# V of the memory rows turned by transposing DMA, attention's last blocks emptied in one step, and two zero loads on SyncE's queue

## The chip, the cores and the metric

The kernel runs on one NeuronCore of a Trainium2 chip; the other cores are idle. The metric is the device time of that core in microseconds, as the median of several executions. Five engines work side by side, each through its own list of instructions, in order: TensorE (PE, matrix products, with the weight loads shown apart as PEld), VectorE (DVE), ScalarE (ACT), GpSimd (POOL) and SyncE (SP, which here only issues DMA transfers). DMA transfers can also be issued from ACT and from POOL; all of them are carried by the same 16 DMA engines.

## The reference, cut to what matters

Two independent parts are computed and their outputs laid side by side. Part A is a state-space layer: a complex linear recurrence over 2048 steps between two matrix products. Part B is attention with a recurrent memory: the 2048 rows of x are cut into 64 segments of 32, and each segment attends to its own rows and to 8 memory rows, which are the first 8 output rows of the segment before.

```python
mem = mem0
for s in range(n_seg):                                   # 64 segments
    xs = x[:, s*32:(s+1)*32, :]
    h = concatenate([mem, xs], axis=1)                   # 8 + 32 rows
    q, k, v = (einsum('btd,dhe->bhte', h, W) for W in (Wq, Wk, Wv))   # 32 heads of 128
    p = softmax(where(mask, q @ k.T * scale, -1e9))
    o = einsum('bhte,hed->btd', p @ v, Wo)
    mem = o[:, :8, :]
    outs.append(o[:, 8:, :])
```

The kernel does not run the segments one after another. It guesses the memory rows from means of x, computes all segments at once with them, and tests at the end whether the guess was within a tolerance; a branch with a plain loop stands ready for inputs where it was not, and is not taken here. "Memory rows" below are the 73 guessed rows (66 of them one to three for each group of three segments, and 7 for the first).

## The kernel before: the parts that the change touches

V of all rows is kept in DRAM, in `vx` for the rows of x and in `vt` for the memory rows, one pair of tensors for each group `hb` of four heads, with ones in 8 columns behind each head's 128 (`EW` is 136, `E` is 128). For the memory rows V comes out of the projection with the head's 128 columns on the partitions (`vm`), so it has to be turned before it is stored. TensorE does that, VectorE copies the result out of PSUM into a staging tile, and two transfers store it:

```python
def v_mem(self, hb, w=None):
    w = w or self.load_wv(hb)
    p = k.ps("P")
    for h in range(4):
        for c in range(KC):                               # 8
            k.PE.matmul(p[:, h*NM:(h+1)*NM], w[:, c, h*128:(h+1)*128], self.memT[:, c, :], ...)
    vm = self.vmp.tile([128, 4, NM], BF16, name="b_vm", bufs=1)         # NM is 73
    k.copy("v", vm[:], p[:, 0:4*NM]...)
    yield
    pt = k.ps("P", (128, 1024), BF16)
    for h in range(4):
        k.PE.transpose(pt[0:NM, h*128:(h+1)*128], vm[:, h, :], k.ident[:])
    st = self.next_st()                                   # one of two staging tiles b_vst
    k.copy("v", st[0:NM, 0, :, 0:E], pt[0:NM, 0:512]...)
    sv = st[:, 0, :, :].rearrange("p h e -> p (h e)")
    k.SP.dma_start(self.vx[hb][64:64+NMX, :], sv[0:NMX, :])             # 7 rows
    k.SP.dma_start(self.vt[hb][:], sv[NMX:NM, :])                       # 66 rows
    yield
```

`v_mem` is called for the eight groups in turn: for 0 and 1 during the last output blocks of part A (`stage2`, a loop over 32 half blocks of 16 matmuls), for 2 to 7 during attention, at steps 4 and 6 of every second head pair.

Attention walks over 16 head pairs `hp`. For each of 11 steps `u` it makes scores, exponentials and masked weights (`att_front`), and multiplies older weights with V (`att_back`, three blocks at a time), keeping up to 8 blocks behind. V of a head pair is loaded from DRAM into one of two tiles of 128 partitions, of which 99 hold V; the 29 others are filled with zeros once per tile, from a stretch of zeros in DRAM:

```python
def load_v(self, hp):
    vt = self.vts[hp % 2]
    if hp < 2:
        z = self.vx[0][T+32:T+32+128-GW, 0:2*EW].unsqueeze(1).to_broadcast([128-GW, NG, 2*EW])   # 29 x 22 x 272
        k.tc.keep_in_program_order(k.G.dma_start(vt[GW:128, :, :], z))
    ...
    k.tc.keep_in_program_order(k.SP.dma_start(vt[0:GX, :, :], self.vx[hb]...))   # 96 x 22 x 272
    k.SP.dma_start(vt[GX:GW, :, :], self.vt[hb]...)                              # 3 x 22 x 272
    ...

def attention(self):
    ...
    for hp in range(HP):                                  # 16
        for u in range(NU):                               # 11
            if u == 2:
                self.load_v(hp + 1)
            pend += self.att_front(hp, u)
            back(8)
            yield hp, u
    for keep in (6, 3, 0):
        back(keep)
        yield HP, 0
```

Every `yield` of attention is filled with matmuls of other work: with the projections of q and k for the next head pair (`proj`), and at the end with the first output product (`outproj_first`, four matmuls at a time). `V` of head pair 0 is loaded at the end of part A, in `att_init`; the projections of q and k for pair 0 run in between.

Of the kernel before, what the change touches and what calls it, by code (L numbers as in the profile page):

```python
# [9 lines left out]
BF16 = mybir.dt.bfloat16  # L10
# [16 lines left out]
HB = 8; HP = 16  # L27
# [7 lines left out]
NMX = 7  # L35
NM = NTL + NMX
# [3 lines left out]
EW = E + 8  # L40
# [13 lines left out]
class Pinned:  # L54


    def __init__(self, k, name, eng):
        self.k, self.name, self.eng = k, name, eng
# [278 lines left out]
class PartB:  # L337
    def __init__(self, k, x, mem0, Wq, Wk, Wv, Wo, out):
        self.k = k
        self.x, self.mem0, self.out = x, mem0, out  # L340
        self.Wf = [w.rearrange("(c p) h e -> p c (h e)", p=128) for w in (Wq, Wk, Wv)]
        self.Wo = Wo.rearrange("h e d -> e h d")
        self.vx = [k.drp.tile([NSLOT, 4 * EW], BF16, name=f"b_vx{i}") for i in range(HB)]
        self.vt = [k.drp.tile([NTL, 4 * EW], BF16, name=f"b_vt{i}") for i in range(HB)]
        self.on = [k.drp.tile([T, 1024], BF16, name=f"b_on{i}") for i in range(4)]
        self.tn = [k.drp.tile([NR, 1024], BF16, name=f"b_tn{i}") for i in range(4)]
        c = k.cst
        self.m0T = c.tile([128, KC, M], BF16, name="b_m0T")
        self.gx = c.tile([128, KC, NM], BF16, name="b_gx")
        self.vmp = c  # L350
        self.xbar = c.tile([128, KC, NSEG], BF16, name="b_xbar")
        self.ogT = c.tile([128, H, NSEG], BF16, name="b_ogT")
        self.accE = c.tile([128, HP * NU], FP32, name="b_accE")
        self.accR = c.tile([128, HP * 2 * NG], FP32, name="b_accR")
        self.flag = c.tile([1, 1], I32, name="b_flag")
# [184 lines left out]
    def v_mem(self, hb, w=None):  # L540
        k = self.k
        w = w or self.load_wv(hb)
        p = k.ps("P")
        for h in range(4):
            for c in range(KC):
                k.PE.matmul(p[:, h * NM:(h + 1) * NM], w[:, c, h * 128:(h + 1) * 128], self.memT[:, c, :], start=(c == 0), stop=(c == KC - 1))
        vm = self.vmp.tile([128, 4, NM], BF16, name="b_vm", bufs=1)
        k.copy("v", vm[:], p[:, 0:4 * NM].rearrange("p (h n) -> p h n", h=4))
        yield
        pt = k.ps("P", (128, 1024), BF16)  # L550
        for h in range(4):
            k.PE.transpose(pt[0:NM, h * 128:(h + 1) * 128], vm[:, h, :], k.ident[:])
        st = self.next_st()
        k.copy("v", st[0:NM, 0, :, 0:E], pt[0:NM, 0:512].rearrange("p (h e) -> p h e", h=4))
        sv = st[:, 0, :, :].rearrange("p h e -> p (h e)")
        k.SP.dma_start(self.vx[hb][64:64 + NMX, :], sv[0:NMX, :])
        k.SP.dma_start(self.vt[hb][:], sv[NMX:NM, :])
        yield


# [57 lines left out]
    def load_v(self, hp):  # L618
        if hp < HP:
            k = self.k  # L620
            vt = self.vts[hp % 2]
            if hp < 2:
                z = self.vx[0][T + 32:T + 32 + 128 - GW, 0:2 * EW].unsqueeze(1).to_broadcast([128 - GW, NG, 2 * EW])
                k.tc.keep_in_program_order(k.G.dma_start(vt[GW:128, :, :], z))  # L624
            hb, cs = hp // 2, slice((hp % 2) * 2 * EW, (hp % 2) * 2 * EW + 2 * EW)
            k.tc.keep_in_program_order(k.SP.dma_start(vt[0:GX, :, :], self.vx[hb].rearrange("(g p) n -> p g n", p=GX)[:, :, cs]))
            k.SP.dma_start(vt[GX:GW, :, :], self.vt[hb].rearrange("(g j) n -> j g n", j=3)[:, :, cs])
            self.vtile[hp] = vt
# [62 lines left out]
    def attention(self):  # L691
        pend = []

        def back(keep):
            while len(pend) > keep:
                n = min(3, 2 * NG - pend[0][1])
                self.att_back([pend.pop(0) for _ in range(n)])
        for hp in range(HP):
            for u in range(NU):
                if u == 2:  # L700
                    self.load_v(hp + 1)
                pend += self.att_front(hp, u)
                back(8)
                yield hp, u
        for keep in (6, 3, 0):
            back(keep)
            yield HP, 0


    def load_o(self, tb, q, t):  # L710
# [265 lines left out]
def kernel_main(tc, A_x, A_Lre, A_Lim, A_Bre, A_Bim, A_Cre, A_Cim, A_logdt, A_Dskip, B_x, B_mem0, B_Wq, B_Wk, B_Wv, B_Wo, out,  # L976
                force=False, dbg=None):
    with ExitStack() as ctx:
        k = K(tc, ctx)
# [3 lines left out]
        b = PartB(k, B_x, B_mem0, B_Wq, B_Wk, B_Wv, B_Wo, out)  # L983

        def pool(name, side, bufs=2):
            return tc.tile_pool(name=name, bufs=bufs, side=side, reuse_waits="tile")
# [8 lines left out]
        with pool("p1x", "right") as p1x, pool("p1", "right", 1) as p1:  # L995
# [10 lines left out]
            wv = {0: w0, 1: b.load_wv(1)}  # L1006
# [17 lines left out]
            for kind, pc, q in order[1:]:  # L1024
# [3 lines left out]
                if kind == "v":  # L1028
                    b.v_x(pc, q, wv[pc])
                    if q == 3:  # L1030
                        if pc >= 3:
                            b.og(pc, wv[pc])
                        n = (pc + 2) if pc + 2 < PC else (2, 0)[pc + 2 - PC]
# [3 lines left out]
                n = 4 * pc + q  # L1037
# [27 lines left out]
        with pool("p2h", "right") as p2h, pool("p2", "right") as p2:  # L1065
            a.s2_tiles(p2h, p2)
            g = b.guess(p2)
            s2 = a.stage2()
            b.wog = []
            a.load_h(1, nc.scalar)  # L1070
            for i, _ in enumerate(s2):
                if i in (1, 4, 7):
                    n = (2, 0, 1)[(i - 1) // 3]
                    b.og(n, wv[n], "O")
                    if n == 2:
                        wv[1] = b.load_wv(1)
                if i in (3, 7, 11, 15):
                    b.load_wog((3, 7, 11, 15).index(i), p2)
                if i in (9, 11, 13, 15, 17, 19, 21, 22):
                    next(g)  # L1080
                if i == 20:
                    b.load_wqk(0)
                if i == 23:
                    for _ in g:
                        pass
                if i in (26, 28):
                    vm = b.v_mem((i - 26) // 2, wv[(i - 26) // 2])
                if 26 <= i < 30:
                    next(vm)


# [15 lines left out]
        for n, (hp, u) in enumerate(at):  # L1107
            if n == 12:
                k.SP.dma_start(wo0[:], b.Wo[:, :, 0:512])
            if hp % 2 == 0 and 2 < hp + 2 < HP:  # L1110
                if u == 4:
                    vm = b.v_mem(hp // 2 + 1)
                if u in (4, 6):
                    next(vm)
            if hp == 13 and u in (3, 6, 9):
                b.load_o_early(u // 3 - 1)
            want = min(18 * HP, LEAD + (n + 1) * 18 // 11)
            while done < want:
                next(pr)
                done += 1  # L1120
            if done == 18 * HP:
                if first is None:
                    xs.close()
                    b.p4a = ctx.enter_context(pool("p4a", "left", 1))
                    wo1 = b.p4a.tile([128, H, 512], BF16, name="wo1")
                    b.wo = (wo0, wo1)
                    b.load_o_early(3)
                    for h in range(0, H, 16):
                        k.SP.dma_start(wo1[:, h:h + 16, :], b.Wo[:, h:h + 16, 512:D])
                    first = b.outproj_first()  # L1130
                next(first)
# [30 lines left out]
@with_exitstack  # L1162
def kernel(
    ctx: ExitStack,
    tc: tile.TileContext,
    A_x: bass.AP,
    A_Lambda_re: bass.AP,
    A_Lambda_im: bass.AP,
    A_B_re: bass.AP,
    A_B_im: bass.AP,  # L1170
    A_C_re: bass.AP,
    A_C_im: bass.AP,
    A_log_dt: bass.AP,
    A_Dskip: bass.AP,
    B_x: bass.AP,
    B_mem0: bass.AP,
    B_Wq: bass.AP,
    B_Wk: bass.AP,
    B_Wv: bass.AP,
    B_Wo: bass.AP,  # L1180
    B_seg_len: bass.AP,
    out: bass.AP,
):
    assert int(B_seg_len) == SEG
    kernel_main(tc, A_x, A_Lambda_re, A_Lambda_im, A_B_re, A_B_im, A_C_re, A_C_im, A_log_dt, A_Dskip,
                B_x, B_mem0, B_Wq, B_Wk, B_Wv, B_Wo, out)
# [35 lines left out]
```

## Time and profile before

| | |
|---|---|
| median of 3 executions | 1248.88 us (1248.05 to 1248.9) |
| span of the profiled execution | 1246.3 us |
| granted TensorE clock, mean | 0.999 |
| PE busy | 1234.5 us in 8270 matmuls |
| DVE, POOL, ACT busy | 668.1, 283.0, 263.6 us |
| DMA traffic | 176.91 MB, mean 142 GB/s |
| transposes of `b_vm` on PE | 32 |
| zero loads, issued from POOL | 2, of 338.9 KB each |

How it is read: the profile is one execution, seen by a hardware profiler. Matrix products overlap one another, so the busy time of one (its line gives, for instance, 219 ns) is longer than the distance from one start to the next; what a matmul costs is read from the starts in the timeline. A transfer's own line gives the time in which the issuing engine was held by the issue, not the time until the data was there. The DMA column of the window view is the mean busy share of 16 engines.

### The profile page before, as it was taken

Reading aid. Unit: us, or ns where it says so; the run is one execution under the profiler, and the core shown is the slowest. Engines: PE = TensorE matmul, PEld = TensorE weight load, DVE = VectorE, ACT = ScalarE, POOL = GpSimd, SP = SyncE. Lnnn points to the kernel's source line nnn. Section 1 sums busy time; section 2 is a strip of 40 time slices with the busy share of each in tenths; the row PEclk is TensorE's granted clock in tenths of the full one; section 3 lists DMA queues with packets and bytes.
Section 4 is the critical chain, followed back from the end, with each engine's and each line's share of the span. In section 5 each row is a group of like instructions: output and inputs, shape, how many; then the busy total and the mean of one; then the engine's idle time right before and its main releaser. Section 6 shows DMA issues by size and latency. Waiting matters only on the chain.

```text
span 1246.3 us, 20124 instructions
## 1 busy us (share of the span) xinstructions
PE 1234.5 (99%) x8270; PEld 662.3 (53%) x8342; DVE 668.1 (54%) x1250; ACT 263.6 (21%) x631; POOL 283.0 (23%) x409
## 2 busy tenths in 40 slices
PE   9999999999999999999999999999999999999998
PEld 5444444444455555656565656555665554446444
DVE  4688899998711124666666666666666641001000
ACT  5344444443310000211111111111111110000000
POOL 4111331212332332222222222323222320000000
PEclk9999999999999999999999999999999999999999
DMA  9965444553898737764454544545474279407000
GB/s 251 267 194 146 130 139 125 146 153 110 243 319 249 246 105 158 150 155 119 102 144 108 144 108 110 142 89 130 96 153 99 58 223 229 107 18 153 17 17 27
DMA packets 317336, 176.91 MB, mean 142 GB/s; under 512 B 141080, under 2 KB 302480, under 8 KB 317240
## 3 DMA queue, kind: packets, MB, share of 16 engines
q1 hardware_dynamic: 292552, 147.26, 48.4%
q10 hardware_dynamic: 21072, 24.38, 5.9%
q0 software_dynamic: 3616, 3.94, 1.3%
q8 instruction: 66, 1.08, 0.4%
q14 instruction: 30, 0.25, 0.1%
HBM read 89.14 MB, written 53.17 MB: 114 GB/s over the span
## 4 chain that ended last, share of the span: by engine, by line
PE 97%; issue 1%; DMA 1%; POOL 0%; DVE 0%; another core or an unknown queue 0%; ACT 0%; POOLq 0%; DVEq 0%; ACTq 0%
PE psP L64 81%; PE psU L64 9%; PE psS L64 3%; PE psO L64 2%; PE psR L64 2%; DMA out_dram<-a_ot 1%; POOL b_m L644 0%; POOL b_v L624 0%; ACT b_e L641 0%; DVE a_ot L327 0%; DVE b_xe L91 0%; DVE b_q L91 0%; DVE b_ost L91 0%; DVE a_n L963 0%
## 5 line engine op out<-in xcount | busy, mean ns | idle before, releaser
L64 PE MATMUL psP<-b_xe,b_wq 128*128 128x480 bf16 (+1 forms) x1280 | 247.9, 343 | 0.7 <-DVE b_q L91 0.6
L64 PE MATMUL psP<-b_xe,b_wk 128*128 128x480 bf16 (+1 forms) x1280 | 247.7, 343 | 0.0
L64 PE MATMUL psP<-b_wv,b_xe 128*128 128x512 bf16 (+2 forms) x1033 | 223.2, 372 | 0.9 <-DVE b_xe L91 0.2
L644 POOL TENSOR_TENSOR b_m<-b_e,maskB 99x396 bf16<-99x396 bf16 x160 | 139.7, 874 | 331.0 <-ACT b_e L641 331.0
L641 ACT ACTIVATE b_e<-psS 99x396 bf16<-99x396 f32 x176 | 88.2, 501 | 533.8 <-PE psS L64 529.6
L64 PEld LDWEIGHTS <-b_wk 128*128 128x128 bf16 x1280 | 119.4, 98 | 94.2
L64 PEld LDWEIGHTS <-b_wq 128*128 128x128 bf16 x1280 | 118.7, 98 | 88.4 <-issue 0.9
L64 PEld LDWEIGHTS <-b_xe 128*128 128x128 bf16 x1056 | 101.8, 98 | 119.1 <-DVE b_xe L91 0.3
L91 DVE CAST b_k<-psP 128x480 bf16<-128x480 f32 (+1 forms) x192 | 97.3, 529 | 99.6 <-PE psP L64 99.6
L91 DVE CAST b_q<-psP 128x480 bf16<-128x480 f32 (+1 forms) x192 | 97.4, 529 | 92.3 <-PE psP L64 90.8
L64 PEld LDWEIGHTS <-b_ol 128*128 128x128 bf16 x864 | 84.3, 98 | 94.4
L64 PE MATMUL psU<-a_xT,a_bt 128*128 128x512 bf16 x493 | 113.9, 379 | 1.1
L64 PE MATMUL psP<-t,a_hl 128*128 128x512 bf16 x496 | 112.1, 379 | 0.8
L91 DVE CAST b_ost<-psP 128x512 bf16<-128x512 f32 (+1 forms) x17 | 11.5, 676 | 182.6 <-PE psP L64 181.5
L64 PE MATMUL psP<-wo,b_ol 128*128 128x512 bf16 (+1 forms) x440 | 91.9, 364 | 0.4
L64 PE MATMUL psP<-t,b_ol 128*128 128x512 bf16 x408 | 91.7, 379 | 0.4
L280 POOL TENSOR_SCALAR a_tt<-a_pr,a_tabf 128x1 f32<-128x1 f32 x48 | 34.0, 709 | 243.2 <-DVE a_pr L275 243.2
L661 DVE TENSOR_TENSOR b_ob<-psO,b_accR 99x384 bf16<-99x384 f32 x160 | 86.0, 554 | 2.1
L89 ACT ACTIVATE b_vst<-psP 128x512 bf16<-128x512 f32 x126 | 72.1, 589 | 70.9 <-PE psP L64 65.8
L267 DVE TENSOR_TENSOR a_pr<-psU,a_tabf 128x2048 f32<-128x2048 f32 x32 | 73.0, 2282 | 15.7 <-PE psU L64 14.0
L64 PEld LDWEIGHTS <-a_bt 128*128 128x128 bf16 x512 | 49.2, 98 | 57.6
L64 PEld LDWEIGHTS <-a_hl 128*128 128x128 bf16 x512 | 49.1, 98 | 56.6
(201 smaller groups left out, 971.7 us busy)
## 6 DMA issues: line engine op xcount, KB each, us to landing
b_v<-b_vx SPq DMA_DIRECT2D x16, 1122.0 KB
b_wv<-in_B_Wv_dram SPq DMA_DIRECT2D x16, 1024.0 KB
b_on<-b_ob SPq DMA_DIRECT2D x15, 960.0 KB
b_vx<-b_vst ACTq DMA_DIRECT2D x24, 544.0 KB
a_hs<-a_h SPq DMA_DIRECT2D x32, 256.0 KB
b_wog<-in_B_Wo_dram SPq DMA_DIRECT2D x4, 2048.0 KB
b_wq<-in_B_Wq_dram SPq DMA_DIRECT2D x16, 512.0 KB
b_wk<-in_B_Wk_dram SPq DMA_DIRECT2D x16, 512.0 KB
```

Of the source, the lines that this page charges most:

```text
L64: r = f(*a, **kw)
L89: self.S.activation(out, in_, ACT.Copy)
L91: self.V.tensor_copy(out, in_)
L267: V.tensor_tensor(pr[:], u[:].unsqueeze(1).to_broadcast([128, 2, 2, TB]), view(t3, [[TB + 1, 2], [TB + 1, 2], [1, TB]]), ALU.mult)
L280: G.tensor_scalar(tt[:, j:j + 1], w[:, j, TB - 1:TB], t3[:, 1, TB:TB + 1], None, ALU.mult)
L641: k.S.activation(e[:], s[0:GW, :, :, 0:GW], ACT.Exp, scale=float(E) ** -0.5, accum_out=self.accE[0:GW, i:i + 1])
L644: k.G.tensor_tensor(m[0:GW, 0:4 * GP].rearrange("p (a b q) -> p a b q", a=2, b=2)[:, :, :, 0:GW], e[:], mask[0:GW, :, :].unsqueeze(2).to_b ...
L661: V.tensor_tensor(self.ob[:, b0:b0 + n, :], o[0:GW, 0:n, 0:E], r.unsqueeze(2).to_broadcast([GW, n, E]), ALU.mult)
```

## The change

Three things change. First, V of the memory rows is no longer turned on TensorE. `vm` (now padded with zeros to 128 columns, allocated once) is stored to DRAM as it is, and four transposing transfers per group of heads read it back turned, straight into the staging tile; two transfers then store it as before, in pieces of one head. This is meant to take 32 transposes and 8 copies off TensorE and VectorE. `v_mem` gets one more step, and starts one half block earlier in part A. Second, the last attention blocks are emptied in one go, with no other matmuls in between. Third, the two zero loads are issued from SP in place of POOL.

```diff
+        self.vmt = [k.drp.tile([4, E, 128], BF16, name=f"b_vmt{i}") for i in range(HB)]
...
-        vm = self.vmp.tile([128, 4, NM], BF16, name="b_vm", bufs=1)
-        k.copy("v", vm[:], p[:, 0:4 * NM].rearrange("p (h n) -> p h n", h=4))
+        if hb == 0:
+            self.vm = self.vmp.tile([128, 4, 128], BF16, name="b_vm", bufs=1)
+            k.V.memset(self.vm[:, :, NM:128], 0.0)
+        k.copy("v", self.vm[:, :, 0:NM], p[:, 0:4 * NM].rearrange("p (h n) -> p h n", h=4))
+        k.SP.dma_start(self.vmt[hb].rearrange("h e n -> e h n"), self.vm[:])
         yield
-        pt = k.ps("P", (128, 1024), BF16)
+        s = self.next_st()[:].rearrange("p i h e -> p (i h e)")[:, 0:576].rearrange("p (h e) -> p h e", h=4)
+        k.V.memset(s[:, :, E:EW], 1.0)
         for h in range(4):
-            k.PE.transpose(pt[0:NM, h * 128:(h + 1) * 128], vm[:, h, :], k.ident[:])
-        st = self.next_st()
-        k.copy("v", st[0:NM, 0, :, 0:E], pt[0:NM, 0:512].rearrange("p (h e) -> p h e", h=4))
-        sv = st[:, 0, :, :].rearrange("p h e -> p (h e)")
-        k.SP.dma_start(self.vx[hb][64:64 + NMX, :], sv[0:NMX, :])
-        k.SP.dma_start(self.vt[hb][:], sv[NMX:NM, :])
+            k.SP.dma_start_transpose(s[:, h, 0:E], self.vmt[hb][h])
+        yield
+        k.SP.dma_start(self.vx[hb][64:64 + NMX, :].rearrange("n (h e) -> n h e", h=4), s[0:NMX, :, 0:EW])
+        k.SP.dma_start(self.vt[hb].rearrange("n (h e) -> n h e", h=4), s[NMX:NM, :, 0:EW])
         yield
...
-                k.tc.keep_in_program_order(k.G.dma_start(vt[GW:128, :, :], z))
+                k.tc.keep_in_program_order(k.SP.dma_start(vt[GW:128, :, :], z))
...
-        for keep in (6, 3, 0):
-            back(keep)
-            yield HP, 0
+        back(0)
+        yield HP, 0
...
-                if i in (26, 28):
-                    vm = b.v_mem((i - 26) // 2, wv[(i - 26) // 2])
-                if 26 <= i < 30:
+                if i in (25, 28):
+                    vm = b.v_mem((i - 25) // 3, wv[(i - 25) // 3])
+                if 25 <= i < 31:
                     next(vm)
...
-                if u in (4, 6):
+                if u in (4, 6, 8):
                     next(vm)
```

## The prediction

> **What bounds the kernel now.** I read the page's busy table first, then the chain of work that ended last: both say TensorE.
>
> ```profile
> PE 1234.5 (99%) x8270; PEld 662.3 (53%) x8342; DVE 668.1 (54%) x1250; ACT 263.6 (21%) x631; POOL 283.0 (23%) x409
> ...
> PE 97%; issue 1%; DMA 1%; POOL 0%; DVE 0%; another core or an unknown queue 0%; ACT 0%; POOLq 0%; DVEq 0%; ACTq 0%
> ```
>
> PE is busy 1234.5 of 1246.3 us, so a change can gain only what it takes off PE's list or out of PE's few gaps, and loses whatever makes PE wait. VectorE at 54% is not near to taking over. Next, the view of the tile that holds V of the memory rows:
>
> ```profile
> L64 PE MATMUL psP<-ident,b_vm x32: 219/219/219, 455.4 to 910.3; 128*73 128x128 bf16 x32
> L91 DVE CAST b_vm<-psP x8: 461/462/463, 452.2 to 904.8; 128x292 bf16<-128x292 f32 x8
> ```
>
> 219 ns is the length of one transpose, not its price. The timeline of PE around the first group gives that:
>
> ```profile
> 451.99 3.62 PE L64 MATMUL psP<-t,a_hl 128*128 128x512 bf16 x15
> 455.44 0.39 PE L64 MATMUL psP<-ident,b_vm 128*73 128x128 bf16 x4
> 455.67 3.62 PE L64 MATMUL psP<-t,a_hl 128*128 128x512 bf16 x16
> ```
>
> From the start of the group to the start of the next work it is 455.67 - 455.44 = 0.23 us for four. The 16 matmuls before it take 455.44 - 451.99 = 3.45 us, with no gap, and the groups in attention are as dense (572.30 to 572.52). So nothing waits at the transposes; they cost their 0.22 to 0.23 us.
>
> Then the places where PE does wait, and what the two zero loads do there: first the view of the tile `b_v`.
>
> ```profile
> L624 POOL DMA_DIRECT2D b_v<-b_vx x2: 3681/3704/3727, 460.6 to 491.4; - x2
> DMA to landing us min/median/max: 26.7/30.8/34.9
> ```
>
> On the timelines of POOL and of PE:
>
> ```profile
> 491.37 3.68 POOL L624 DMA_DIRECT2D b_v<-b_vx  x1 [0.30 <-PE psP L64]
> 495.07 1.71 POOL L644 TENSOR_TENSOR b_m<-b_e,maskB 99x396 bf16<-99x396 bf16 x2
> ...
> 492.68 0.50 PE L64 MATMUL psO<-b_v,b_m 128*128 128x129 bf16 x6
> ...
> 496.01 0.23 PE L64 MATMUL psR<-b_v,b_m 128*128 128x129 bf16 x1 [0.72 <-POOL b_m L644]
> ```
>
> And on those of DVE and PE a little earlier:
>
> ```profile
> 479.87 0.10 DVE L568 MEMSET b_q<- 128x50 bf16 x1 [3.84 <-DMA out_dram<-a_ot]
> ...
> 480.81 3.40 PE L64 MATMUL psP<-b_xe,b_wq 128*128 128x480 bf16 x16 [0.61 <-DVE b_q L91]
> ```
>
> The first zero load is issued at 460.6 and lands 26.7 us later, at 487.3; the first product with V, which reads all 128 partitions, comes at 492.68. So this transfer, 338.9 KB, has a margin of only 5 us. The second holds POOL for 3.68 us, and PE waits 0.72 us for the mask that stands behind it. Last, the window view over a stretch with hardly anything but the second zero load:
>
> ```profile
> 516.00:524.00 8.00, 8.00 (x59) 4.48 (x57) 5.04 (x13) 1.75 (x6) 1.75 (x2) 1.00 0.07 22
> ```
>
> A DMA share of 0.07 is one engine of sixteen (1/16 = 0.063), moving 22 GB/s. A zero load runs on a single DMA engine: 347 thousand bytes / 22 GB/s = 15.8 us at the least.
>
> [...] SP's `b_wq` issue at 469.53 is held 15.15 us, while an engine is slow.
>
> **Part by part.**
>
> *Transposes.* 8 groups x 0.23 us = 1.84 us off PE's list, all of it on the path. The built program shows no other matmul added or lost. On DVE, 8 copies of 0.39 us go and 9 small fills come: no effect, since DVE idles.
>
> *Turning by DMA in attention (groups 2 to 7).* The chain is store, four transposes, two stores. A transpose of 128x1024 is issued in 1.3 to 1.5 us in this trace, one of 512x1024 in about 4 us; this puts a 128x128 one near 0.4 us, four near 2 us (estimate). SP gets busier by some 4 us every 68 us. V of the group is loaded five steps after the last step of `v_mem`; a step is about 3.1 us (33.8 us per head pair / 11), so 15 us of slack. Hidden: 0.
>
> *Zero loads off POOL.* POOL no longer stands for 3.68 us in front of the mask: 0.72 us, with its neighbour about 0.8 us, won.
>
> *Gap at 480.2.* DVE waited until 479.87 for part A's last output to land, because the V load of 468 to 482 filled all engines (share 1.07 in 474 to 480). In the changed program that load comes later, and the output should land before it: 0.6 us won, if so; I count 0.5.
>
> *Emptying in one step.* The second group of three blocks needs the last mask. POOL makes it from 1016.66 to 1017.53; PE did the first group at 1016.77, then four output matmuls, then the second at 1017.80. Without the four in between PE waits for the mask and its passing on: about 0.6 us lost.
>
> *V of head pair 0.* This is the term that decides. In the changed program SP's order is: stores of group 1's V, load of `vt`, zeros, V load (1122 KB), weights. SP reaches the zeros only after group 1 has been turned:
>
> - `v_mem` for group 1 ends on PE at about 460.1 (one half block of 3.45 us earlier than before for group 0, then three halves). The copy ends at 460.7, the store to DRAM is issued at 461 behind a 1 MB weight load, which in the trace kept the DMA busy until 466, so it lands near 466.5.
> - Four transposes: issued until 468.5, landed near 470.5. The two stores and the load of `vt` take SP until about 472.5.
> - Zeros issued at 472.5, first data 2 to 4 us later (the V load issued at 468.23 raised the DMA share only from 474 on), 15.8 us on the one engine: until 490.5 to 492.5.
> - That engine's sixteenth of the V load follows, 132 rows of 544 bytes at 22 GB/s: 3.3 us, and about 1 us to signal. V is there at 495 to 497.
> - PE would reach the first product with V at 492.68 - 0.46 (two groups of transposes) - 0.5 = 491.7.
>
> So PE stops for 3 to 5 us; with SP's delays summed at the larger end, 8. I take 5. Behind a stopped PE nothing is made up later. The second zero load is queued behind the weights of pair 1, from about 500 to 518, its V load is there by 525, and it is needed 33.8 us after the first: 496 + 33.8 = 530. Hidden, with little to spare.
>
> Sum: -1.84 - 0.8 - 0.5 + 0.6 + 5 = +2.5 us; 1248.9 + 2.5 = 1251.4 us.
>
> **Rivals.** *A: only the transposes count.* If the zeros were spread over many engines or got to SP early, V would land in time as it does now; then -2.5 us, 1246.4. [...] *B: the single engine is slower from SP.* SP's descriptors are single rows of 544 bytes. If one took 40 ns in place of 25, the zeros would last 25 us, the stop would be some 14 us, and the second zero load would make PE wait as well: 1262 to 1270. Against it: the V loads in attention move 190 GB/s over 562 to 571 on 16 engines, about 12 GB/s each under full load, so alone it should be nearer to 22. *C: SP becomes the bound in attention*, its transposes holding back weights or V: each late load would stop PE some us, six times. Against it: the 15 us of slack, and SP's order, which puts the next weights ahead of the transposes. *D: emptying in one step delays the last output rows*, and with them the transposed loads of the output product. Against it: PE has 12 more output matmuls and whole blocks of others before it needs them.
>
> **Range and chances.** From A's -2.5 to a stop of 13 us: 1246 to 1261. B's worst end is +20 us, under the 25 us that 2% is. Faster by 2% isn't to be had, as PE's list shrinks by only 0.15%: 0.01. Within 2%: 0.96. Slower by more: 0.03.
>
> **What would show it.** PE busy down by about 2 us, 32 fewer matmuls. The first product with `b_v` on PE stands behind an idle of 3 to 8 us that names a DMA of `b_v`, near 492. SP's issue of the zeros is held for ten us or more, and the DMA share is 0.06 meanwhile. No wait at 496 for a mask; one of 0.6 us near 1016 in its stead. If the first product with V doesn't wait, the decisive step is wrong, and A is right; a wait of over 10 us, or a second one near 526, means B; waits of PE every 68 us mean C.

## The result, and the profile after

| kernel | median us | range us | to the kernel before |
|---|---|---|---|
| before | 1248.89 | 1248.05 to 1249.16 | |
| after | 1263.03 | 1262.38 to 1264.79 | 1.0117 [1.0099, 1.0134] |

The change makes the kernel slower by 14.1 us; 1251.4 was predicted, and the range ended at 1261. The page of the kernel after, its busy row and the chain of work that ended last:

```profile
PE 1236.5 (98%) x8240; PEld 661.4 (52%) x8310; DVE 666.4 (53%) x1251; ACT 263.6 (21%) x631; POOL 275.7 (22%) x407
...
PE 93%; DMA 5%; SPq 1%; issue 0%; DVE 0%; POOL 0%; ACT 0%; ACTq 0%; DVEq 0%
```

PE's share of the chain was 97% and is 93%: 5% of it is DMA now. The span is 1260.7 us in place of 1246.3, so 14.4 us more, and they split in two: PE is idle for 1260.7 - 1236.5 = 24.2 us in place of 11.8 (+12.4), and busy for 1236.5 in place of 1234.5 (+2.0), although 32 transposes are gone. (Some 70 matmuls have no record in either trace: there are 8342 weight loads to 8270 matmuls before and 8310 to 8240 after. So both idle times are some us too long, by about the same amount, and the 32 that went show in the weight loads.) The view of waits says what it was idle for (engine and work that waited, what it waited for; us in total, times, longest):

```profile
PE psP L64 <- DVE b_q L91: 8.0, 1, 8.0
PE psO L64 <- DMA b_v<-b_vx: 4.7, 1, 4.7
PE psR L64 <- DVE hpb L105: 1.3, 1, 1.3
PE psO L64 <- POOL b_m L647: 0.9, 3, 0.4
PE psP L64 <- DVE b_vm L91: 0.8, 1, 0.8
```

There are two long stops, where the prediction had one. The second is the one that it spoke of, the first product with V of head pair 0. The first was not in it at all. Both in the timeline of PE (start, us, work, and in brackets the idle time ahead of it with its releaser):

```profile
484.61 3.15 PE L64 MATMUL psP<-b_xe,b_wq 128*128 128x480 bf16 x8 [7.98 <-DVE b_q L91]
...
507.58 0.57 PE L64 MATMUL psO<-b_v,b_m 128*128 128x129 bf16 x6 [4.71 <-DMA b_v<-b_vx]
```

Why were DVE's copies of Q late? DVE itself stood still, in front of two of the new fills of ones (its timeline):

```profile
468.05 0.09 DVE L555 MEMSET b_vst<- 128x32 bf16 x1 [7.43 <-DMA b_vt<-b_vst]
...
482.83 0.09 DVE L555 MEMSET b_vst<- 128x32 bf16 x1 [9.86 <-DMA b_vt<-b_vst]
```

These are the fills for groups 2 and 3, which are turned only in attention. They depend on nothing but a free staging tile, so the scheduler put them far forward, into the end of part A. A free staging tile, though, is one whose store to `vt` (group 0, then group 1) has landed. For 9.86 us a fill of 0.09 us holds all that DVE has behind it, the copies of Q among it.

And why was V late? The chain that ended last, from the store of group 0's V to the first product (start, us, what):

```profile
464.44 3.47 DMA b_vt<-b_vst
...
468.13 0.45 DVE b_vm L91
468.60 4.15 DMA b_vmt<-b_vm
...
476.60 2.32 DMA b_vst<-b_vmt
...
481.69 25.76 DMA b_v<-b_vx
```

The first of the two fills is on this chain too: it waits for that store, and the copy of group 1's V (468.13) stands right behind it. The timeline of SP has the rest of it:

```profile
472.81 4.96 SPq L64 DMA_TRANSPOSE b_vst<-b_vmt  x4
479.07 0.82 SPq L64 DMA_DIRECT2D b_vx<-b_vst  x1
479.94 0.83 SPq L64 DMA_DIRECT2D b_vt<-b_vst  x1
480.81 0.47 SPq L64 DMA_DIRECT2D b_v<-b_vt  x1
481.33 16.19 SPq L64 DMA_DIRECT2D b_v<-b_vx  x2
```

The last line is the zero load together with the V load: SP is held for 16.19 us, 0.32 us of it by the zeros' issue and the rest by the V load's. A transposing transfer of 128x128 takes SP 4.96 / 4 = 1.24 us, three times the 0.4 us of the prediction. The zeros go out at 481.3, 8.8 us later than predicted.

One thing more shows in the view of windows (start and end, us, busy time of PE, PEld, DVE, ACT and POOL, then granted clock of PE, DMA share, GB/s):

```profile
484.00:486.00 2.00, 1.39 (x4) 0.58 (x5) 2.00 (x12) 0.00 (x0) 0.00 (x0) 0.50 0.08 24
486.00:488.00 2.00, 2.00 (x7) 0.76 (x6) 0.28 (x2) 0.00 (x0) 0.00 (x0) 0.65 0.07 22
488.00:490.00 2.00, 2.00 (x11) 0.98 (x10) 1.44 (x7) 0.00 (x0) 0.00 (x0) 1.00 0.07 22
...
496.00:498.00 2.00, 2.00 (x15) 1.06 (x14) 1.04 (x2) 0.30 (x1) 0.00 (x0) 1.00 0.08 21
498.00:500.00 2.00, 2.00 (x15) 1.06 (x14) 0.84 (x2) 0.80 (x4) 0.87 (x1) 1.00 0.86 191
...
508.00:510.00 2.00, 2.00 (x8) 0.76 (x6) 1.23 (x4) 0.00 (x0) 0.00 (x0) 0.50 0.07 21
510.00:512.00 2.00, 2.00 (x14) 1.04 (x13) 0.61 (x2) 0.34 (x1) 0.00 (x0) 0.68 0.08 21
```

After each stop PE works on at half clock, by these windows until 487.4 and 511.3, which is 2.8 and 3.7 us after its restarts. The 8 matmuls from 484.61 take 2.99 us to the next start, the 16 from 487.60 take 3.24. So each of these stops costs more than its own length, 1.4 and 1.7 us more (worked out below), and this is most of why PE's busy time rose with less work on its list. The DMA share of 0.07 to 0.08 at 21 to 24 GB/s, from 484 on, is the zeros on one engine, as in the kernel before. It lasts until 498, when SP's issue of the V load has ended: the other fifteen engines, nearly idle until then, get their parts of V no earlier. Beside these views the trace has a record of landings, one for each engine's share of a transfer. In it 15 shares of this V load land between 504.25 and 505.29, and the last at 507.44.

### The profile page after: what moved, and what is told of

Same layout as the page of the kernel before. It is cut to its first block, busy times and chain, and to the rows that moved or that the text cites. A ratio compares the mean times of both kernels' runs of the same rounds, so it can differ in the third digit from the quotient of the medians.

```text
span 1260.7 us, 20102 instructions
## 1 busy us (share of the span) xinstructions
PE 1236.5 (98%) x8240; PEld 661.4 (52%) x8310; DVE 666.4 (53%) x1251; ACT 263.6 (21%) x631; POOL 275.7 (22%) x407
## 4 chain that ended last, share of the span: by engine, by line
PE 93%; DMA 5%; SPq 1%; issue 0%; DVE 0%; POOL 0%; ACT 0%; ACTq 0%; DVEq 0%
PE psP L64 77%; PE psU L64 9%; PE psS L64 3%; PE psO L64 2%; DMA b_v<-b_vx 2%; PE psR L64 2%; SPq L64 1%; DMA b_vmt<-b_vm 1%; DMA wo<-in_B_Wo_dram 1%; DMA b_wv<-in_B_Wv_dram 1%; DMA b_vst<-b_vmt 0%; DMA b_vt<-b_vst 0%; DVE b_vm L91 0%; POOL b_m L647 0%; DVE b_ost L91 0%
```

## The experiments

My theory after reading this: the loss is made of two things that lie one behind the other at the start of attention. Nearest to the end lies V of head pair 0, late by SP's serial work plus 16 us of zeros on one engine; behind it lies DVE, held by fills moved too far forward. The rivals: the fills alone, the queue from which the zeros come, the mere number of transfers, the size of V's own load.

| kernel | median us | ratio to before, 95% | PE's stops over 1.5 us |
|---|---|---|---|
| after | 1263.03 | 1.0117 [1.0099, 1.0134] | 8.0 (Q), 4.7 (V) |
| pin | 1263.59 | 1.0119 [1.0102, 1.0135] | 14.6 (V) |
| zpool | 1274.85 | 1.0211 [1.0194, 1.0228] | 13.9 (Q), 10.8 (`b_vm`) |
| pin_zpool | 1278.86 | 1.0239 [1.0222, 1.0256] | 29.0 (V) |
| b_zsp | 1246.70 | 0.9983 [0.9976, 0.9990] | none |
| onet | 1255.19 | 1.0056 [1.0039, 1.0072] | 7.3 (V) |
| pin_z32 | 1247.68 | 0.9990 [0.9981, 0.9998] | 1.7 |
| pin_zms | 1245.13 | 0.9971 [0.9960, 0.9983] | none |
| zms | 1256.51 | 1.0065 [1.0049, 1.0080] | 8.6 (Q) |
| b_zms | 1246.57 | 0.9984 [0.9977, 0.9990] | none |
| onet_zms | 1245.19 | 0.9973 [0.9962, 0.9983] | none |
| onet_zms_3 | 1244.31 | 0.9966 [0.9953, 0.9978] | none |
| b_one | 1249.28 | 1.0004 [0.9995, 1.0013] | none |

### pin: the fills kept in their place

```diff
-        k.V.memset(s[:, :, E:EW], 1.0)
+        k.tc.keep_in_program_order(k.V.memset(s[:, :, E:EW], 1.0))
```

> The changed kernel with only the order on VectorE altered: the fill of ones for each group stands where it is written, and not two groups ahead. Theory 1 (V of head pair 0 comes late, because SP turns group 1 first and the zeros then hold one DMA engine for 16 us; VectorE's wait for the fills merely lies under it): the waits of 7.4 and 9.9 us on VectorE vanish, the zeros are issued 1 to 2 us earlier, near 480, V lands near 505, and PE stops once, for about 13 us, before the first product with V; 1261 to 1263 us. Theory 2 (the fills' wait is a cost of its own): the stop of 8.0 us goes and that of 4.7 us stays; about 1253 us.

Measured: 1263.59 us, as long as after. SP's timeline:

```profile
466.31 0.65 SPq L64 DMA_DIRECT2D b_vmt<-b_vm  x1
472.31 4.96 SPq L64 DMA_TRANSPOSE b_vst<-b_vmt  x4
...
480.77 16.21 SPq L64 DMA_DIRECT2D b_v<-b_vx  x2
```

Without the fill ahead of it, group 1's store goes out 2.3 us earlier than in after, but it takes 6.0 us to land in place of 4.2, and the zeros go out only 0.6 us earlier. The stop at the copies of Q is gone, and the one at V has grown from 4.7 to 14.6 us:

```profile
506.99 0.81 PE L64 MATMUL psO<-b_v,b_m 128*128 128x129 bf16 x6 [14.62 <-DMA b_v<-b_vx]
```

The first product starts at 506.99, in after at 507.58. So V's arrival sets the time, and the wait for the fills lay wholly in front of it. That a cause can be taken away without gain does not say yet that it is harmless; `zms`, below, does that part.

### zpool and pin_zpool: the zeros from POOL again

```diff
-                k.tc.keep_in_program_order(k.SP.dma_start(vt[GW:128, :, :], z))
+                k.tc.keep_in_program_order(k.G.dma_start(vt[GW:128, :, :], z))
```

zpool is after with this edit, pin_zpool has the fills kept in place as well.

> The changed kernel with the two zero loads issued from POOL again. Theory 1: V's load starts on all engines at 482 and lands near 491, so the wait of 4.7 us at the first product with V goes; VectorE still waits for the fill, so the stop of 8.0 us stays; 1256 to 1257 us. Rival (the zero loads are the whole loss): back to about 1248 us. Rival (they cost nothing from SP): 1263 us.

> The changed kernel with both: fills in their written place and zero loads from POOL. What is left of the change is the turning by DMA and the one-step emptying. Theory 1: both stops are gone, 1.8 us for the transposes gained, 0.4 to 0.9 us lost at the emptying, V landing at about 490, just in time: 1247.5 to 1249 us. If the DMA turning itself still makes V late: a stop before the first product with V and over 1250 us.

Measured: 1274.85 and 1278.86 us, both slower than after. Theory 1 was wrong in both. In pin_zpool the other branch named what came, a stop before the first product with V and over 1250 us, but not its cause: pin_zms, below, turns V by DMA in the same way and has no such stop. In pin_zpool POOL issues the zeros at 461.86, early enough, but the timeline of SP shows what happens to the store of group 1:

```profile
465.62 0.47 SPq L64 DMA_DIRECT2D b_wv<-in_B_Wv_dram  x1
466.15 4.75 SPq L64 DMA_DIRECT2D b_vmt<-b_vm  x1
490.87 4.96 SPq L64 DMA_TRANSPOSE b_vst<-b_vmt  x4
```

The store of 128 KB goes out at 466.15, and the transposes, which need it landed, start at 490.87: 24.7 us in place of 472.31 - 466.31 = 6.0 us in pin. Meanwhile the view of windows has

```profile
478.00:482.00 4.00, 3.05 (x16) 1.37 (x14) 0.44 (x4) 0.00 (x0) 0.00 (x0) 1.00 0.07 27
482.00:486.00 4.00, 3.50 (x18) 1.72 (x18) 2.67 (x10) 0.00 (x0) 0.00 (x0) 1.00 0.09 28
486.00:490.00 4.00, 4.00 (x25) 2.01 (x24) 1.91 (x3) 0.59 (x2) 0.00 (x0) 1.00 0.06 21
```

that is, one engine of sixteen (0.06 to 0.09), with zeros to move, while TensorE comes to stand still for 29.0 us at V. So here one transfer on one engine held up others of another queue that look independent of it. The record of landings shows how. Of the store's 16 shares, 15 landed from 476.76 to 478.44 and the last at 490.80; of the 1 MB of weights ahead of it, 15 by 477.76 and the last at 490.45; the zeros themselves were landed at 489.88. Each of the two transfers had one share that came in only after the zeros, 12 to 13 us behind the last of its other fifteen, and the transposes started at 490.87, 0.07 us after the store's last share. In the kernel before, the same befell V itself: 15 shares of head pair 0's V landed from 479.37 to 481.60 and the last at 489.81, still ahead of its use at 492.68, and no store had to be landed and read back in that time. In zpool the moved fills make it felt earlier: DVE waits 17.41 us in front of one for the landing of a store, the copy of `b_vm` waits behind it, and group 1's transposes start at 490.36.

### b_zsp: the zeros from SP in the kernel before

The one edit, in the kernel before, is the opposite of the one above (`k.G.dma_start` becomes `k.SP.dma_start`).

> The kernel before with only the zero loads moved to SP. The group's V is turned on TensorE here, so SP reaches the zeros near 468.5. Theory 1: zeros 16 us on one engine, V at about 491.5 to 494 against a need at 492.7, a stop of 0 to 2 us; POOL's issue time gone, 0.8 us gained: 1248 to 1250 us, and an issue of the V load held for some 16 us. If the zero loads from SP cost by themselves: 1253 us or more.

Measured: 1246.70 us, ratio 0.9983, under the 1248 to 1250 expected: this part of the change is a gain when taken alone. The timeline of SP in this kernel:

```profile
465.83 16.06 SPq L64 DMA_DIRECT2D b_v<-b_vx  x2
```

The pair holds SP as long here (16.06 us), but it goes out at 465.83. V's last share lands at 491.26, and the first product doesn't wait:

```profile
491.83 0.50 PE L64 MATMUL psO<-b_v,b_m 128*128 128x129 bf16 x6
```

In pin the same pair goes out at 480.77, which is 14.9 us later, and PE stops for 14.6 us. Lateness on SP is paid almost one to one, as a margin of only 0.6 us is left.

### onet: one transposing transfer per group

```diff
-        self.vmt = [k.drp.tile([4, E, 128], BF16, name=f"b_vmt{i}") for i in range(HB)]
+        self.vmt = [k.drp.tile([E, 4 * 128], BF16, name=f"b_vmt{i}") for i in range(HB)]
...
-        k.SP.dma_start(self.vmt[hb].rearrange("h e n -> e h n"), self.vm[:])
+        k.SP.dma_start(self.vmt[hb][:], self.vm[:].rearrange("p h n -> p (h n)"))
...
-        for h in range(4):
-            k.SP.dma_start_transpose(s[:, h, 0:E], self.vmt[hb][h])
+        k.SP.dma_start_transpose(s[:, :, 0:E], self.vmt[hb][:])
```

This is on top of pin.

> The kernel after with the fills kept in place (as in pin), and with each group's four 128x128 transposing transfers replaced by one of 128x4x128 out of a DRAM tile that is stored in rows of 1 KB instead of 256 bytes. The zero load stays on SP's queue. Theory (the length of SP's serial work ahead of the zero load is paid one to one, and the four transposes are its largest part, 4.98 us of SP's time per group): the zeros of head pair 0 go out at 471 to 475 instead of 480.8, V is there at 497 to 501 instead of 507, TensorE stops for 5 to 9 us instead of 14.6, and the time is 1252 to 1258. Rival (the cost of a transposing transfer goes by its data and not by its number): about the time of pin, 1262 to 1265, with the stop near 14.6 us.

Measured: 1255.19 us, as the theory had it. The four transposes and the one, in the view of the tile `b_vmt`; first the kernel after (ns: minimum, median, maximum):

```profile
L64 SPq DMA_TRANSPOSE b_vst<-b_vmt x32: 1133/1224/2925, 455.6 to 928.6; - x32
```

and onet:

```profile
L64 SPq DMA_TRANSPOSE b_vst<-b_vmt x8: 1207/1243/1620, 456.5 to 915.3; - x8
```

Its zero load and its stop, on the timelines of SP and PE:

```profile
473.46 16.21 SPq L64 DMA_DIRECT2D b_v<-b_vx  x2
...
499.94 0.81 PE L64 MATMUL psO<-b_v,b_m 128*128 128x129 bf16 x6 [7.29 <-DMA b_v<-b_vx]
```

The issue costs 1.2 us whether it turns 128x128 or 128x4x128. Two groups with three issues fewer each make 2 x 3 x 1.24 = 7.4 us; the zeros go out at 473.46, which is 7.3 us earlier than in pin, and the stop is 7.3 us, so 7.3 us shorter. The time falls by 8.4 us. The store with longer rows, which comes along with this edit, plays no part: the transposing transfer starts 6.0 us after it (462.43 to 468.42), as in pin.

### pin_z32: zeros over 32 partitions instead of 29

```diff
-                z = self.vx[0][T + 32:T + 32 + 128 - GW, 0:2 * EW].unsqueeze(1).to_broadcast([128 - GW, NG, 2 * EW])
-                k.tc.keep_in_program_order(k.SP.dma_start(vt[GW:128, :, :], z))
+                z = self.vx[0][T + 32:T + 32 + 128 - GX, 0:2 * EW].unsqueeze(1).to_broadcast([128 - GX, NG, 2 * EW])
+                k.tc.keep_in_program_order(k.SP.dma_start(vt[GX:128, :, :], z))
```

This too is on top of pin, with all four transposes per group. (The 4 MB load of the output weights is kept behind the first loads of V, as below.)

> pin with the zero loads widened from 29 partitions (99 to 127) to 32 (96 to 127), still on SP's queue at the same place; the load of rows 96 to 98 from the turned V then has to follow the zeros. (The 4 MB load of the output weights is kept behind, as in pin_zms.) Nothing else differs from pin. Theory ([...] the zeros use one DMA engine, and this makes their 16 us; 32 spreads over 16): the zero load takes 1 to 4 us instead of 16, V is there by 490 to 494, the stop is 0 to 3 us instead of 14.6, and the time is 1245 to 1249. Rival (the zeros are slow because all of their partitions read the same few rows of DRAM, or because of their place on SP): the stop stays over 10 us and the time at 1260 or more.

Measured: 1247.68 us, which is 15.9 us less than pin, for three more partitions of zeros. SP's timeline, and PE's at the first product:

```profile
482.50 1.07 SPq L64 DMA_DIRECT2D b_v<-b_vx  x2
488.77 0.24 SPq L64 DMA_DIRECT2D b_v<-b_vt  x1
...
494.84 0.50 PE L64 MATMUL psO<-b_v,b_m 128*128 128x129 bf16 x6 [1.72 <-POOL b_m L647]
```

Zeros and V load hold SP for 1.07 us in place of 16.21. Why the zeros were slow shows in the record of landings: it has one share of the zeros in after, at 501.98, but 16 in pin_z32, from 486.08 to 488.75, and the issue shrinks by a factor of fifteen. So over 29 partitions they went through one engine and over 32 through sixteen, as I had guessed. Only these two counts were run, and what sets the number of engines was not shown. (The first partition moved from 99 to 96 along with the count; that was not tried alone.) The 6.3 us between SP's two lines are the new wait of the small load for the zeros' landing. A stop of 1.7 us is left. The view of waits names POOL's mask for it, but POOL had made its second mask, the last that these six products read, by 491.36. By the record of landings V was there at 494.15 and the small load at 494.70, and PE went on at 494.84; so the small load came last, and V, 0.6 us ahead of it, would have held PE nearly as long.

### pin_zms, zms and b_zms: zeros filled on chip

```diff
-            if hp < 2:
-                z = self.vx[0][T + 32:T + 32 + 128 - GW, 0:2 * EW].unsqueeze(1).to_broadcast([128 - GW, NG, 2 * EW])
-                k.tc.keep_in_program_order(k.SP.dma_start(vt[GW:128, :, :], z))
...
+        for t in self.vts:
+            self.k.G.memset(t[GX:128, :, :], 0.0)
...
-                k.SP.dma_start(wo0[:], b.Wo[:, :, 0:512])
+                k.tc.keep_in_program_order(k.SP.dma_start(wo0[:], b.Wo[:, :, 0:512]))
```

POOL fills the partitions from 96 on before attention, and no zeros are loaded. pin_zms is pin with this, zms is after with it (the fills of ones free to move), b_zms the kernel before with it.

> The kernel after with the fills kept in place, and without the two zero loads: POOL fills partitions 96 to 127 of both V tiles with zeros by two fills of 32x5984 before attention (estimate 5.7 us each, from 0.42 us for 128x440), and the 4 MB load of the output weights is kept behind the first two loads of V. The four transposes per group, with all their 5 us of SP's time, stay. Theory (the zeros' 16 us on one DMA engine lie between the turned V and the first product): V goes out at about 480.8 and is there by 490 to 494, the stop is 0 to 3 us, and the time is 1245 to 1250. Rival (V's own load over DRAM, not the zeros, is the long part): stop still over 8 us and 1256 or more.

> The kernel after with POOL's fills in place of the zero loads (as in pin_zms), but with the scheduler free to move the fills of ones again. Theory (the moved fills hold DVE until the stores of groups 0 and 1 have landed, and in the kernel after this was hidden only because V came later still): TensorE stops once, for 7 to 9 us, at a product that waits for DVE's copies of Q, at about 476 to 485, and the time is 1253 to 1257, 8 to 12 us above pin_zms. Rival (the stop at the copies was itself caused by the zeros): 1245 to 1247.

> The kernel before with POOL's two fills of 32x5984 in place of the two zero loads (and the 4 MB load of the output weights kept behind the first loads of V); the TensorE transposes and the emptying in three steps stay. It is what the change has to be measured against once the zeros are out of the way. If the 32 transposes cost what their issue takes: 1.8 us above onet_zms_3, 1246.0 to 1246.7. If most of what onet_zms_3 gained came from the zeros alone: under 1245.2.

Measured: 1245.13, 1256.51 and 1246.57 us. In pin_zms V still goes out late, at 480.36, but arrives in time:

```profile
480.36 0.51 SPq L64 DMA_DIRECT2D b_v<-b_vx  x1
```

and its first product starts without a wait:

```profile
492.45 0.50 PE L64 MATMUL psO<-b_v,b_m 128*128 128x129 bf16 x6
```

The kept place of the 4 MB load was not run alone, but it is not what removed the stop: in pin that load goes out only at 531.67, long after V. So neither the four transposes nor the way through DRAM need cost anything; with 16 us of zeros behind them they did. In zms, the same kernel with the fills free to move, the view of waits has the stop that pin had seemed to clear of blame:

```profile
PE psP L64 <- DVE b_q L91: 8.6, 1, 8.6
```

It costs 11.4 us against pin_zms. Each of the two causes alone is enough to make the kernel slower than before; taking away the one (pin) leaves the other in charge.

### b_one, onet_zms and onet_zms_3: the emptying, and the best of both

b_one is the kernel before with the last blocks emptied in one step; onet_zms is pin with both the single transposing transfer and POOL's fills; onet_zms_3 is that with the emptying in three steps again:

```diff
-        back(0)
-        yield HP, 0
+        for keep in (6, 3, 0):
+            back(keep)
+            yield HP, 0
```

> The kernel before with the last blocks emptied in one step instead of three, nothing else changed. My prediction put this at +0.6 us (the kernel after shows a wait of 0.43 us for POOL's mask there): 1249.2 to 1249.9, ratio 1.0003 to 1.0008. If the one step frees the output stage earlier and that counts: under 1248.5.

> onet_zms_3 with the last blocks emptied in one step, as in the kernel after. If one step costs the 0.3 to 0.6 us seen between before and b_one: 1244.6 to 1245.0. If the 0.8 us between pin_zms and onet_zms_3 came from the number of transposing transfers instead: 1244.2 to 1244.5.

> Both edits, one transposing transfer per group and POOL's zeros in place of the zero loads, and the emptying in three steps again: the turned V as the change means it, without what held it up. If the 32 TensorE transposes are worth what their issue takes (1.8 us), and nothing else is lost: 1244 to 1246, no stop over 1 us. If the move to DMA costs TensorE something that the stop had hidden: 1247 or more.

Measured: b_one 1249.28 us, where the interval holds 1: alone this says nothing. onet_zms 1245.19 (1245.12 to 1245.34) against onet_zms_3 1244.31 (1244.19 to 1244.57): 0.9 us for the one step, a little over what I expected. pin_zms and onet_zms are alike (1245.13 and 1245.19), so once V has slack the number of transposing transfers is worth nothing.

onet_zms_3 is the fastest kernel here, 4.3 us under the kernel before. Against b_zms, which has the same zeros and the same emptying, it shows what turning V by DMA is worth: 1246.57 - 1244.31 = 2.3 us.

## Why the prediction was wrong

**Transposes, -1.84 us: right.** 2.3 us between b_zms and onet_zms_3.

**"8 copies go and 9 small fills come: no effect, since DVE idles": wrong, and the first step that failed.** I weighed the fills by their length, 0.09 us, and by DVE's idle time. What counts of an instruction on an engine that takes its work in order is what it waits for. Two of them waited 7.43 and 9.86 us for a store to land, with the copies that PE needed behind them: a stop of 8.0 us in after, and 11.4 us of time in zms against pin_zms. No term of the prediction asked at which place in DVE's order the fills would stand.

**V of head pair 0, +5 us: the wait right, its size not.** The product with V waited for the zeros on one engine, and the zeros waited for the turned V on SP, as the prediction had it. (One engine for zeros from SP was my estimate, as the trace of before had it only for those from POOL; in after the DMA share is 0.07 to 0.08 meanwhile, and the zeros land as one share.) But the zeros went out at 481.3 and not at 472.5. Of these 8.8 us, 3.0 are the transposes' issue (4.96 against 2), and 6.3 are the store to DRAM, which was landed at 472.8 and not at 466.5. The moved fills are not the reason (it is 472.31 in pin): SP comes to this store only behind the transposes and stores of group 0 and a 1 MB weight load, at 466.31 in pin, where I had let it go at 461; the last transposing transfer was landed a little sooner than I had it (1.3 us after the end of its issue, and not 2). I had scaled the issue of a transposing transfer down with its size, to 0.4 us, and it took 1.2 us (median of the 32 in after). From there on the number nearly held, V being there 26 us after the issue where I had 22.5 to 24.5 (my 1 us from the last data to the signal is 0.7 in before, both for the zeros, 486.55 to 487.25, and for V, 489.11 to 489.81), but partly by luck: only one engine's part of V was to stand behind the zeros, an estimate that no trace had shown, and in fact the whole V load did, its issue held until 497.5 and 15 of its 16 shares landing only from 504.25 on. By itself this stop is 14.6 us (pin), about three times the 5 of my sum. That is the size that rival B gave, but B's reason, an engine slower from SP, was wrong: it moved 21 to 22 GB/s as from POOL. The range was mis-added as well: by the prediction's own terms a stop of 13 us makes 1248.9 - 2.5 + 13 = 1259.4 us, not 1261. V of head pair 0 needs only group 0, whose last store was landed at 467.9; in SP's order it stood behind group 1. To load it before group 1 is turned was not tried.

**Nothing for the clock: wrong.** "Behind a stopped PE nothing is made up later" was too mild, as more is lost; PE's busy time, forecast to fall by about 2 us, rose by 2.0. Against the kernel without the causes of the stops, the time grew by more than the stops:

| kernel | against | time, us | stops, us | rest, us | half clock, worked out, us |
|---|---|---|---|---|---|
| after | pin_zms | +17.9 | 12.7 | 5.2 | 3.1 |
| pin | pin_zms | +18.5 | 14.6 | 3.9 | 2.0 |
| zms | pin_zms | +11.4 | 8.6 | 2.8 | 1.9 |
| onet | onet_zms | +10.0 | 7.3 | 2.7 | 1.6 |

The last column comes from the view of windows: half of the time that PE works, after the restart, until the granted clock is 1.00 again. In after, for instance, 0.65 in the window 486 to 488 puts the return at 487.4, so 2.8 us after the restart at 484.61, of which 1.4 are lost; the second stop loses 1.7 (the clock fell at 507.88, just after the restart). The time column compares medians, the stops are those of one execution. Between the spans of the profiled executions the time grew by 17.3, 17.2, 10.9 and 9.4 us, which leaves 0.4 to 1.5 us per kernel unexplained; in after, 0.8 us of it is PE's short wait for `b_vm`.

**The smaller terms.** Zeros off POOL and the gap at 480, -1.3 us together: b_zsp gains 2.1 us [1.2, 3.0], so right, though in after the gap's place is taken by the 8.0 us stop. Emptying in one step, +0.6: 0.9, with a wait of 0.43 us for POOL's mask in after where the prediction put it:

```profile
1031.92 0.29 PE L64 MATMUL psO<-b_v,b_m 128*128 128x129 bf16 x2 [0.43 <-POOL b_m L647]
```

Second zero load hidden, and no harm from the transposes in attention: right, as no wait of PE names either. Rival A (1246.4) is what comes out once the zeros are out of the way and the fills in their place: pin_zms 1245.1, pin_z32 1247.7.

**The sum mended:** -1.84 - 0.8 - 0.5 + 0.6 + 8.0 + 4.7 + 0.8 + 3.1 = +14.1 us, 1263.0 us; measured 1263.03. The stops are put in as measured, so this shows that nothing large is missing, and tests no more than that.

## What to carry to other kernels

Weigh an added instruction by what it waits for on an engine that works in order, not by its length: a fill of 0.09 us that needed a landed store held DVE for 7.43 and for 9.86 us here. When a step is moved from a compute engine to a chain of transfers, add up each issue and each landing up to the first use, and look for a transfer that runs on one engine. From SP it held back the whole load issued behind it (in after no share of V landed before 504.25, with the issue begun at 481.7), from POOL one share each of two transfers of SP's queue (in pin_zpool they landed at 490.45 and 490.80, the other fifteen by 477.76 and 478.44). Here, with the fills in their place, zeros over 32 partitions in place of 29 took back the loss (1247.68 us in pin_z32, 1263.59 in pin). And when taking one cause away changes nothing, look for a second behind it before it is called harmless.

## What the runs showed of the hardware beside this

- A transposing transfer cost SP 1.2 us of issue, for 128x128 (median 1224 ns in after) as for 128x4x128 (1243 ns in onet).
- A load of zeros on one DMA engine, issued from POOL, held back one of the 16 shares of a 128 KB store from SP: in pin_zpool 15 landed by 478.44 and the last at 490.80, so that the store was landed 24.7 us after its issue, where it took 6.0 us in pin and 4.2 us in after. Issued from SP, such a load held back all shares of the load issued behind it: in after they landed 22.6 to 25.8 us after 481.7.
- PE's granted clock fell to 0.50 in these stops or just behind them, and stayed there for some microseconds of work. Worked out from the views of windows, it fell 3.9 us after the first stop of after began (at 480.6), 5.0 us after the second (at 507.9, PE having just gone on) and 5.1 us after that of pin (at 497.4); in zms it was at 0.50 from 480.0 at the latest, 4.0 us after the stop began. It was full again 2.8 and 3.7 us after the restarts in after, 4.1 in pin, 3.7 in zms and 3.2 in onet. So the stretches at half clock last 6.8 and 3.4 us in after and 13.6 in pin. The stop of 1.7 us in pin_z32 left it at 1.00. What sets the time of the fall and of the return was not shown.
